# Hand-given SyncE order, a spectrum kept in SBUF, direct weight loads and deeper rings in a spectral-mixer and token-MLP kernel

## The chip, the core and the metric

The kernel runs on one core of a Trainium2 chip. The metric is the device time of one execution in microseconds, and a smaller number is better. The core's engines are TensorE (PE, the matrix unit), VectorE (DVE), ScalarE (ACT), GpSimd (POOL) and SyncE (SP). Here SyncE issues every data transfer. All transfers run on the core's 16 DMA engines.

## What is computed

The program computes a forward pass of two residual blocks and all its gradients except that of a constant input. The first block mixes with a two-dimensional real FFT of a normalised input of 2048 by 448, multiplied by a learned complex filter. The second is a token-mixing MLP across the 2048 rows.

```python
def _A_ref(x, w_r, w_i):
    X = jnp.fft.rfft2(x.astype(jnp.float32), axes=(-2, -1))
    X = X * (w_r + 1j * w_i)                    # w: 2048 x 225
    return jnp.fft.irfft2(X, s=(S, D), axes=(-2, -1)).astype(jnp.bfloat16)

def _B_ref(x, w1, b1, w2, b2):                  # w1: 2048 x 1792, w2: 1792 x 2048
    h = _layernorm(x, axis=-1)
    u = _gelu(jnp.einsum("bsd,sf->bdf", h, w1) + b1)
    y = jnp.einsum("bdf,fs->bds", u, w2) + b2
    return y.transpose(0, 2, 1)

h  = x + _A_ref(_layernorm(x), w_r, w_i)
h2 = h + _B_ref(_layernorm(h), w1, b1, w2, b2)
# outputs: h2 (out_0) and the gradients for x (out_1), w_r (out_2), w_i (out_3),
#          w1 (out_4), b1 (out_5), w2 (out_6), b2 (out_7), given grad_out
```

## The kernel before, in words

The transforms are matrix products with cosine and sine tables that the kernel makes at its start on VectorE, ScalarE and GpSimd (`Ut`, `Vt`, `UTt`, `VTt`, `csF`, `csI`, `Rm`, `RTm`). A length of 2048 is split into 16 times 128. The program runs through these stages:

1. **Forward row stage.** `prep_x` folds two of 16 row groups on VectorE, a DMA transpose makes `xT` (line 473), `d_stage` and `s1_stage` multiply it, and a DMA (line 495) writes the result across partitions into `D2`. Between these, `fill(n)` puts n products of `dg_gen` into TensorE's order: the gradient of the MLP's hidden layer, 14 groups of 16 products, each on a transposed block of w2 (line 188).
2. **Forward spectrum stage** (`s2_stage`). For each of eight pairs of groups, TensorE makes the spectrum X, `w_mult` multiplies by the filter on VectorE, and `s2_inv` transforms back. A DMA (line 542) writes the result into `D3`. X is also stored to DRAM (`xspec_d`, line 653), from a ring of two buffers.
3. **Inverse rows** (`inv_rows`) give h row by row, then its layer norm.
4. **u stage** (line 726): seven pairs of blocks of w1 (1 MB each, a ring of two), then the GELU and its derivative.
5. **y stage** (line 771): 16 rows against w2 in 0.9 MB pieces of two rows each (`load_w2c`, line 705, a ring of two).
6. **dh stage** (line 848): 16 rows against transposed blocks of w1 (line 828, a ring of three); the backward row stage runs among its rows (`d_pair`).
7. **Backward spectrum stage** with `bwd_mult`, which also forms the filter's gradient from the stored X and reads the filter from a packed DRAM copy (`w_d`, written at line 656, read at line 858).
8. **Inverse rows of the backward pass** (`gx_consumer`): each row ends in a store of a row group of out_1 (line 944).

From the end of stage 6 to the end, `fill` puts the 480 products of the two weight gradients (`gw2_gen` line 903, `gw1_gen` line 918) between the others. They read transposed slices (line 889, a ring of three, two loaded ahead).

TensorE's order is that of the program text. The order of all other engines, SyncE's included, is set by a scheduler at build time from its own model of time. An engine runs its instructions strictly in that order, so an issue on SyncE that waits holds all that stand behind it. `Ring.next()` gives buffers in turn. The small ring `r448` (8 buffers) holds the row temporaries of `ln_bwd`, so that a row's `tmp` takes the buffer from which the row before was stored.

## Time and profile before

| what | us |
|---|---|
| median of 3 runs | 479.72 (477.13 to 480.07) |
| the profiled execution, its own time | 482.09 |
| its span, first to last instruction | 479.7 |
| TensorE busy in the span (1920 products) | 376.4 |
| VectorE / ScalarE / GpSimd busy | 263.4 / 235.0 / 48.5 |
| moved by DMA | 89.73 MB, 187 GB/s on average |

Busy time is the time in which an engine had an instruction in work. An engine's idle time is put down to what ended it. The granted clock is the share of full speed at which TensorE was let run.

### The profile page before, as it was taken

The numbers are of one execution on the slowest core, as the hardware profiler recorded it, in microseconds if no ns is written. First come the engines' busy times: TensorE is split into PE (matmuls) and PEld (weight loads), VectorE is DVE, ScalarE is ACT, GpSimd is POOL, SyncE is SP. The second block draws the span as 40 slices with busy tenths as digits, with TensorE's granted clock in tenths as the row PEclk, the third lists the DMA queues.
The fourth block names the chain that finished last, engine by engine and source line by source line (L and its number), as shares of the span: only waits on it lengthen the run. The fifth ranks groups of instructions, "written<-read, shape, count | busy, mean of one in ns | idle before, by whom it ended". The sixth has DMA issues, their size and how long they took to land.

```text
span 479.7 us, 6024 instructions
## 1 busy us (share of the span) xinstructions
PE 376.4 (78%) x1920; PEld 190.3 (40%) x1920; DVE 263.4 (55%) x732; ACT 235.0 (49%) x478; POOL 48.5 (10%) x50
## 2 busy tenths in 40 slices
PE   1694577768698999918779899966999998589960
PEld 0252243324353545504335455532444454345530
DVE  9998572642287588821224877700167850235764
ACT  0674532454275545311222234553689885557771
POOL 6105997000000000000000000000000000000000
PEclk9998768979798999987999999997999998979995
DMA  8998969598794674287686999699757869967641
GB/s 230 252 193 175 180 138 265 145 222 209 195 238 183 169 202 139 53 195 194 190 226 113 202 194 195 139 193 287 206 183 209 232 177 223 137 197 168 211 166 57
DMA packets 173255, 89.73 MB, mean 187 GB/s; under 512 B 119081, under 2 KB 168233, under 8 KB 172841
## 3 DMA queue, kind: packets, MB, share of 16 engines
q1 hardware_dynamic: 173224, 89.36, 76.0%
q8 instruction: 15, 0.25, 0.2%
q14 instruction: 16, 0.12, 0.1%
HBM read 29.41 MB, written 25.74 MB: 115 GB/s over the span
## 4 chain that ended last, share of the span: by engine, by line
PE 38%; DMA 27%; DVE 18%; SPq 6%; ACT 4%; POOL 3%; issue 3%; DVEq 0%; ACTq 0%; POOLq 0%
DMA out_dram<-r_81 10%; PE ps_mm L903 8%; PE ps_mm L726 7%; PE ps_mm L848 6%; PE ps_mm L771 3%; PE ps_mm L918 3%; DMA xspec_d<-rS 3%; DVE stats L583 3%; PE ps_mm L603 3%; DMA r_73<-in_B_w_dram 2%; DMA out_dram<-rD 2%; POOL Ut L351 2%; DMA rst<-rE 2%; DVE r_81 L822 2%; SPq L857 2%
## 5 line engine op out<-in xcount | busy, mean ns | idle before, releaser
L603 PE MATMUL ps_mm<-rC,rE 128*128 128x448 bf16 x224 | 60.2, 403 | 14.2 <-DMA rE<-in_B_w_dram 8.0
L918 PE MATMUL ps_mm<-rC,rst 112*128 112x512 bf16 (+1 forms) x256 | 55.6, 367 | 6.3 <-DMA rst<-rB 6.3
L771 PE MATMUL ps_mm<-rE,rS 128*128 128x448 bf16 x224 | 45.2, 362 | 17.2 <-DMA rS<-in_B_w_dram 17.2
L903 PE MATMUL ps_mm<-rG,rst 112*128 112x512 bf16 x224 | 53.9, 390 | 4.2 <-DMA rst<-rE 4.2
L726 PE MATMUL ps_mm<-rB,r_72 128*128 128x448 bf16 x224 | 45.1, 362 | 2.5 <-DVE rB L685 1.7
L848 PE MATMUL ps_mm<-rD,r_73 128*128 128x448 bf16 x224 | 43.7, 352 | 1.1 <-DMA r_73<-in_B_w_dram 1.1
L603 PEld LDWEIGHTS <-rE 128*128 128x128 bf16 x224 | 24.1, 110 | 42.0 <-issue 20.9
L906 ACT CAST rO<-ps_mm 128x512 bf16<-128x512 f32 x56 | 32.0, 594 | 13.0 <-PE ps_mm L903 12.8
L771 PEld LDWEIGHTS <-rS 128*128 128x128 bf16 x224 | 22.0, 100 | 40.2 <-DMA rS<-in_B_w_dram 19.4
L918 PEld LDWEIGHTS <-rst 112*128 112x128 bf16 x256 | 25.1, 101 | 29.5 <-DMA rst<-rB 6.6
L921 ACT CAST rO<-ps_mm 128x512 bf16<-128x512 f32 (+1 forms) x60 | 30.0, 540 | 13.4 <-PE ps_mm L918 13.2
L903 PEld LDWEIGHTS <-rst 112*128 112x128 bf16 x224 | 22.3, 100 | 31.7 <-DMA rst<-rE 4.7
L783 ACT ACTIVATE r_81<-rC 128x448 bf16<-128x448 bf16 x16 | 9.2, 576 | 48.5 <-DVE r_81 L778 38.3
L726 PEld LDWEIGHTS <-r_72 128*128 128x128 bf16 x224 | 22.3, 100 | 25.1 <-issue 4.8
L778 DVE SCALAR_TENSOR_TENSOR r_81<-ps_mm,b2col,r_81 128x448 bf16<-128x448 f32 x16 | 10.8, 682 | 38.1 <-PE ps_mm L771 38.0
L564 PE MATMUL ps_ff<-csI,rAT 113*128 113x448 bf16 x128 | 31.3, 368 | 0.6 <-ACT rAT L553 0.5
L848 PEld LDWEIGHTS <-r_73 128*128 128x128 bf16 x224 | 21.7, 98 | 23.5 <-DMA r_73<-in_B_w_dram 2.2
L480 PE MATMUL ps_ff<-csF,rT 113*128 113x226 bf16 x64 | 13.0, 289 | 17.6 <-DMA rT<-rF 17.6
L553 ACT CAST rAT<-ps_ff 113x512 bf16<-113x512 f32 x32 | 18.4, 584 | 16.6 <-PE ps_ff L550 16.3
L486 ACT CAST r_78<-ps_ff 128x452 bf16<-128x452 f32 x32 | 17.1, 538 | 17.0 <-PE ps_ff L483 17.0
L816 ACT ACTIVATE r_81<-ps_mm 128x448 bf16<-128x448 f32 x16 | 8.7, 544 | 30.0 <-PE ps_mm L848 28.9
L513 ACT CAST rS<-ps_ff 128x452 bf16<-128x452 f32 x29 | 15.7, 540 | 15.1 <-DMA xspec_d<-rS 7.7
(198 smaller groups left out, 609.0 us busy)
## 6 DMA issues: line engine op xcount, KB each, us to landing
r_72<-in_B_w_dram SPq DMA_DIRECT2D x7, 1024.0 KB
rS<-in_B_w_dram SPq DMA_DIRECT2D x8, 896.0 KB
out_dram<-rO SPq DMA_DIRECT2D x14, 512.0 KB
out_dram<-rO SPq DMA_DIRECT2D x16, 448.0 KB
r_72<-r_78 SPq DMA_DIRECT2D x32, 113.0 KB
r_73<-r_78 SPq DMA_DIRECT2D x32, 113.0 KB
out_dram<-r_81 SPq DMA_DIRECT2D x32, 112.0 KB
w_d<-rG SPq DMA_DIRECT2D x1, 1808.0 KB
```

The costliest lines, as they stand in the source:

```text
L486: sc.copy(out=ab, in_=pv)
L513: evac(out=xc[:, i, :, :], in_=pv)
L553: sc.copy(out=aT[0:KC].rearrange("p a b -> p (a b)"), in_=pa[0:KC, :])
L564: nc.tensor.matmul(py[:, 0:D], lhsT=aT[0:KC, i, :], rhs=csI[0:KC, i // 2, i % 2, :], start=(i == 0), stop=(i == 3))
L603: nc.tensor.matmul(pg[:, 0:D], lhsT=wT[:, t, :], rhs=go_tp[:, t, :], start=(t == 0), stop=(t == NT - 1))
L726: nc.tensor.matmul(pu[:, 0:D], lhsT=w1c[:, t, jj * P:(jj + 1) * P], rhs=hln[:, t, :, :], start=(t == 0), stop=(t == NT - 1))
L771: nc.tensor.matmul(py[:, 0:D], lhsT=w2cs[t // 2][:, j, (t % 2) * P:(t % 2 + 1) * P], rhs=g_[:, j, :, :], start=(j == 0), stop=(j == NFB - 1))
L848: nc.tensor.matmul(pdh[:, 0:D], lhsT=wT[:, j, :], rhs=du[:, j, :, :], start=(j == 0), stop=(j == NFB - 1))
L903: nc.tensor.matmul(pw[:], lhsT=gt[0:DC, k, :], rhs=goT[0:DC, k, c * 512:(c + 1) * 512], start=(k == 0), stop=(k == 3))
L906: evac(out=o[:, c * 512:(c + 1) * 512], in_=pw[:])
L918: nc.tensor.matmul(pw[:, 0:n * P], lhsT=ht[0:DC, k, :], rhs=du_t[0:DC, 4 * c:4 * c + n, k, :], start=(k == 0), stop=(k == 3))
L921: evac(out=o[:, c * 512:c * 512 + n * P], in_=pw[:, 0:n * P])
```

## The change

The change takes SyncE out of the scheduler's hands: `manual_schedule` now names PE and SP, so transfers are issued in the order of the program text. To place them, `mm()` replaces every matmul call and adds up columns / 2400 us as a clock of TensorE's work. `defer(us, fn, *views)` puts a transfer into the text once that clock has moved on by `us`, or sooner, when one of its buffers is asked for again. A number of other edits go with it:

- `Xs` in a new region `rX` holds the spectrum from the forward to the backward pass; `xspec_d` and `w_d` are gone. The fold buffers share `rX` in the forward and `rS` in the backward pass, and `s2_stage` takes a lag `ml` (3 forward, 0 backward) between X and its product with the filter.
- The filter's 18 loads (16 partitions by 16 rows of 225 values each, most of them) move from the row stage to the start of the forward spectrum stage. In the backward pass the same 18 loads from `A_w_r` and `A_w_i` replace the one from `w_d`.
- Ring depths: w2's transposed blocks 5 instead of 3, w1's transposed blocks 4 instead of 3, weight-gradient slices 3 loaded ahead instead of 2.
- `grad_out` in its second layout, two w1 blocks and two row groups of h are loaded during the u stage (`after_u`), `goT` in the y stage's later rows, and `du_t` is transposed in four pieces. The filter gradient's 18 stores go out two per row of `gx_consumer`.

```diff
+    def defer(us, fn, *views):
+        ...
+        later.append((clock[0] + us, len(later), run))
+        ...
+        for v in views:
+            Ring.held.setdefault(id(v), []).append(run)
+    def mm(out, lhsT, rhs, start, stop):
+        nc.tensor.matmul(out, lhsT=lhsT, rhs=rhs, start=start, stop=stop)
+        clock[0] += int(np.prod(rhs.shape[1:])) / 2400.0
+        run_due()
-    ctx.enter_context(tc.manual_schedule(engines={mybir.EngineType.PE}))
+    ctx.enter_context(tc.manual_schedule(engines={mybir.EngineType.PE, mybir.EngineType.SP}))
-    w2T_ring = ring(rE, 0, 3, NT, P)
+    w2T_ring = Ring(ring(rE, 0, 3, NT, P).views + ring(rO, S, 2, NT, P).views)
 def dg_gen():
...
                 if t == NT - 1:
                     evac(out=dgu[:, j, :, :], in_=v4(pg[:, 0:D]))
+                    load_w2T()
 def s1_stage(s1, ab):
...
-        nc.sync.dma_start(out=D2[...], in_=cs)
+        defer(RESH_LAG, lambda: nc.sync.dma_start(out=D2[...], in_=cs), cs)
 def s2_stage(get_x, on_mult, ml, n_fill, gap):
+        flush()
...
-        lag = 2
+        lag = 2 + ml
...
-                ys.append(on_mult(c2, xc))
+            if ml <= c2 < nh + ml:
+                ys[c2 - ml] = on_mult(c2 - ml, xs[c2 - ml])
+    def fwd_x(c2):
+        for _ in range(6):
+            next(w_loads, None)
+        return Xs[:, 2 * c2:2 * c2 + 2, :, :]
     def fwd_mult(c2, xc):
-        nc.sync.dma_start(out=xspec_d[:, 2 * c2:2 * c2 + 2, :, :], in_=xc)
         return w_mult(c2, xc, W_view_F, False)
+    after_u = {0: [lambda: load_w2c(0)], 1: [lambda: load_w2c(1)], 2: [lambda: load_go_pt(0)],
+               3: [lambda: load_go_pt(1)], 4: [lambda: load_w1T(0)], 5: [lambda: load_w1T(1)],
+               6: [lambda: load_h(0), lambda: load_h(1)]}
 # y stage, after the products of row t
+        if t % 2 == 1 and t // 2 + 2 < NT // 2:
+            load_w2c(t // 2 + 2)
         y_tail(t, py)
         gb2_part(t)
+        if t in (2, 6):
+            load_w1T(2 + t // 4)
+        if t in (8, 10, 12, 14):
+            load_goT(t // 2 - 4)
-    nc.sync.dma_start_transpose(out=du_t.rearrange("p j b q -> p (j b) q"), in_=rD[:, 0:NFB * 4 * P])
-    nc.sync.dma_start(out=W_view_B, in_=w_d[:])
+    for q in range(4):
+        defer(4.0 * q, lambda q=q: nc.sync.dma_start_transpose(
+            out=du_t.rearrange("p j b q -> p (j b) q")[:, 14 * q:14 * q + 14, :], in_=rD[:, 14 * P * q:14 * P * (q + 1)]))
+    w_back = w_io(W_view_B, A_w_r, A_w_i, False, nc.sync)
+    def bwd_x(c2):
+        if c2 == 0:
+            gp_.memset(W_view_B[:, :, :, DF:KW], 0.0)
+        for _ in range(18):
+            next(w_back, None)
+        return X_ring.next()
     def bwd_mult(c2, xc):
-        xs = xs_ring.next()
-        nc.sync.dma_start(out=xs, in_=xspec_d[:, 2 * c2:2 * c2 + 2, :, :])
+        xs = Xs[:, 2 * c2:2 * c2 + 2, :, :]
 def gx_consumer(t, py):
-        xt = m448.next()
-        nc.sync.dma_start(out=xt, in_=x_pt[:, t, :])
+        for _ in range(2):
+            next(g_out, None)
+        xt = xts.pop(0)
+        if t + 1 < NT:
+            load_xt(t + 1)
...
-        nc.sync.dma_start(out=out_1[0].rearrange(...)[:, t, :], in_=gx)
+        defer(3.5, lambda: nc.sync.dma_start(out=out_1[0].rearrange(...)[:, t, :], in_=gx), gx)
```

**SyncE around the last `D2` stores of the forward row stage.** In the kernel before, `r_72<-r_78` (line 495) are these stores, `rG<-in_A_w` (line 433) the filter's loads, `rT<-rF` (line 473) the `xT` transposes, and `rE<-in_B_w` (line 188) the w2 blocks.

```order
L495 DMA r_72<-r_78 8x16x452
L433 DMA rG<-in_A_w_i_dram 16x16x225
L433 DMA rG<-in_A_w_i_dram 16x225
L495 DMA r_72<-r_78 8x16x452
L473 DMA_TRANSPOSE rT<-rF 128x8x128
L495 DMA r_72<-r_78 8x16x452 x2
L188 DMA_TRANSPOSE rE<-in_B_w_dram 128x16x128
L495 DMA r_72<-r_78 8x16x452 x4
L188 DMA_TRANSPOSE rE<-in_B_w_dram 128x16x128
L495 DMA r_72<-r_78 8x16x452
```

In the changed kernel the same place of SyncE's order reads as follows; line 553 is the `D2` store, line 489 the filter's loads and line 227 the w2 blocks.

```order
L553 DMA r_72<-r_77 8x16x452 x4
L227 DMA_TRANSPOSE rE<-in_B_w_dram 128x16x128
L553 DMA r_72<-r_77 8x16x452 x2
L227 DMA_TRANSPOSE rE<-in_B_w_dram 128x16x128
L489 DMA rG<-in_A_w_r_dram 16x16x225
L489 DMA rG<-in_A_w_r_dram 16x15x225
L489 DMA rG<-in_A_w_r_dram 16x16x225 x6
L489 DMA rG<-in_A_w_r_dram 16x225
L489 DMA rG<-in_A_w_i_dram 16x16x225
```

All 18 loads of the filter, of which the last nine begin here, now stand behind the last `D2` store and one w2 block, in one piece.

**VectorE at the first filter products.** In the kernel before, lines 526 to 530 are one pair's `w_mult`, line 513 is a copy of X out of PSUM, and lines 865 and 867 finish a row of scale factors, `srow`, after a GpSimd memset (line 863).

```order
L499 TENSOR_SCALAR r_72<-r_72 128x4x226 x4
L526 TENSOR_TENSOR rS<-rS,rG 128x904
L527 TENSOR_TENSOR rS<-rS,rG 128x904
L528 TENSOR_TENSOR rS<-rS 128x2x226
L530 TENSOR_TENSOR rS<-rS 128x2x226
L513 CAST rS<-ps_ff 128x452
```

In the changed kernel lines 586 to 590 are that `w_mult`, lines 948 and 950 finish `srow`, and line 962 is the scaling of X by `srow` for the backward pass.

```order
L558 TENSOR_SCALAR r_72<-r_72 128x4x226 x4
L948 TENSOR_TENSOR rO<-rO,srow 128x226
L950 TENSOR_TENSOR srow<-rO 128x226
L586 TENSOR_TENSOR rS<-rX,rG 128x904
L587 TENSOR_TENSOR rS<-rX,rG 128x904
L588 TENSOR_TENSOR rS<-rS 128x2x226
L962 TENSOR_TENSOR rX<-rX,srow 128x904
L590 TENSOR_TENSOR rS<-rS 128x2x226
```

The scaling by `srow` has moved from the backward to the forward spectrum stage, once per pair, and the two instructions that finish `srow` stand ahead of the first product.

**SyncE before the backward spectrum stage.** In the kernel before, `rC<-rD` (line 857) makes `du_t`, `rT<-rF` is the last `xT`, `rD<-w_d` the filter, `out_dram<-rO` (line 908) a store of out_6, and `rst<-rE` (line 889) a weight-gradient slice.

```order
L857 DMA_TRANSPOSE rC<-rD 128x56x128
L473 DMA_TRANSPOSE rT<-rF 128x8x128
L858 DMA rD<-w_d 128x7232
L908 DMA out_dram<-rO 128x2048
L495 DMA r_72<-r_78 8x16x452
L889 DMA_TRANSPOSE rst<-rE 128x4x128
```

In the changed kernel, at the point where the program text enters that stage, line 978 is the slice and line 997 the store of out_6.

```order
L978 DMA_TRANSPOSE rst<-rE 128x4x128
L997 DMA out_dram<-rO 128x2048
L489 DMA rD<-in_A_w_r_dram 16x16x225
L489 DMA rD<-in_A_w_r_dram 16x15x225
L489 DMA rD<-in_A_w_r_dram 16x16x225 x6
L489 DMA rD<-in_A_w_r_dram 16x225
L489 DMA rD<-in_A_w_i_dram 16x16x225
L489 DMA rD<-in_A_w_i_dram 16x15x225
L489 DMA rD<-in_A_w_i_dram 16x16x225 x6
L489 DMA rD<-in_A_w_i_dram 16x225
L978 DMA_TRANSPOSE rst<-rE 128x4x128
L997 DMA out_dram<-rO 128x2048
```

The filter's load has moved from ahead of the first stores of out_6 to behind the sixth, and one instruction has become 18.

## Rows read from the trace of the kernel before

**Rows 1.** Busy time by stage: from:to, length, each engine, PE clock, DMA share, GB/s.

```profile
151.30:195.30 44.00, 43.29 (x217) 21.53 (x217) 30.59 (x78) 23.14 (x31) 0.00 (x0) 0.96 0.57 171
195.30:257.60 62.30, 45.11 (x227) 22.04 (x225) 18.28 (x37) 11.90 (x31) 0.00 (x0) 0.92 0.69 178
257.60:310.20 52.60, 50.30 (x284) 27.33 (x282) 40.20 (x118) 21.21 (x58) 0.00 (x0) 1.00 0.91 176
310.20:347.00 36.80, 27.70 (x123) 12.66 (x122) 3.62 (x11) 19.49 (x37) 0.00 (x0) 0.91 0.90 222
347.00:402.20 55.20, 53.17 (x262) 25.23 (x260) 33.13 (x70) 44.83 (x90) 0.00 (x0) 1.00 0.71 203
402.20:463.40 61.20, 54.90 (x312) 29.64 (x312) 27.84 (x77) 41.08 (x93) 0.00 (x0) 0.92 0.80 179
```

**Rows 2.** Who waited for whom: total us, times, longest us.

```profile
PE ps_mm L771 <- DMA rS<-in_B_w_dram: 17.2, 5, 11.8
...
ACT rS L513 <- DMA xspec_d<-rS: 7.7, 4, 3.6
```

**Rows 3.** SyncE's timeline, forward part: start, us, instruction, how many.

```profile
58.47 1.37 SPq L433 DMA_DIRECT2D rG<-in_A_w_i_dram  x2
...
72.66 1.93 SPq L188 DMA_TRANSPOSE rE<-in_B_w_dram  x1
74.68 0.73 SPq L495 DMA_DIRECT2D r_72<-r_78  x1
```

**Rows 4.** Timelines of ScalarE, GpSimd and VectorE around the forward spectrum stage's start.

```profile
66.54 1.05 ACT L412 ACTIVATE r_73<-r_73 128x448 f32<-128x448 f32 x2 [4.36 <-DVE r_73 L227]
...
80.50 0.28 POOL L863 MEMSET rO<- 128x226 f32 x1
...
82.20 0.63 DVE L526 TENSOR_TENSOR rS<-rS,rG 128x904 bf16<-128x904 bf16 x1 [2.11 <-ACT rS L513]
...
84.02 0.62 DVE L513 CAST rS<-ps_ff 128x452 bf16<-128x452 f32 x1
```

**Rows 5.** The scaling by `srow`, line 873: shortest/median/longest ns, first and last start.

```profile
L873 DVE TENSOR_TENSOR rS<-rS,srow x8: 621/630/630, 255.6 to 384.8; 128x904 bf16<-128x904 bf16 x8
```

**Rows 6.** The chain that ended last, in order of time: start, us, what.

```profile
120.51 4.06 DMA r_73<-r_78
...
212.17 5.56 DMA rS<-in_B_w_dram
...
359.92 1.94 PE ps_mm L903 x9
...
408.14 6.96 DMA out_dram<-rD
```

**Rows 7.** TensorE's timeline around the backward spectrum stage's start: idle before and releaser in brackets.

```profile
324.16 0.56 PE L480 MATMUL ps_ff<-csF,rT 113*128 113x226 bf16 x2 [4.85 <-DMA rT<-rF]
...
334.08 13.05 PE L903 MATMUL ps_mm<-rG,rst 112*128 112x512 bf16 x52 [4.25 <-DMA rst<-rE]
346.97 0.36 PE L511 MATMUL ps_ff<-r_72,Ut 128*128 128x452 bf16 x1
...
356.67 0.35 PE L538 MATMUL ps_ff<-rS,UTt 128*128 128x452 bf16 x1
```

**Rows 8.** SyncE's timeline, backward part.

```profile
312.01 8.88 SPq L857 DMA_TRANSPOSE rC<-rD  x1
...
404.59 8.92 SPq L431 DMA_DIRECT2D out_dram<-rD  x12
```

**Rows 9.** VectorE's timeline: ends of rows 0, 3, 5 and 15 of out_1.

```profile
409.70 0.69 DVE L822 SCALAR_TENSOR_TENSOR r_81<-r_81,rstd_x,rA 128x448 bf16<-128x448 bf16 x1
...
433.16 0.69 DVE L822 SCALAR_TENSOR_TENSOR r_81<-r_81,rstd_x,rA 128x448 bf16<-128x448 bf16 x1
...
441.76 0.69 DVE L822 SCALAR_TENSOR_TENSOR r_81<-r_81,rstd_x,rA 128x448 bf16<-128x448 bf16 x1
...
476.52 0.69 DVE L822 SCALAR_TENSOR_TENSOR r_81<-r_81,rstd_x,rA 128x448 bf16<-128x448 bf16 x1
```

More of the change, by code (lines that the diff above doesn't have):

```diff
@@ L55, in next, with release @@
         self.i += 1
+        Ring.release(v)
         return v
+    @staticmethod
+    def release(v):
+        for run in Ring.held.pop(id(v), ()):
+            run()
 @with_exitstack
```

281 lines of the change are left out of this document (161 added, 120 removed).

## The prediction

> **What bounds the kernel now.** I cut the span into stages first. TensorE is busy 376.4 of 479.7 us, so it is the engine that everything else keeps waiting, and the question for each stage is which wait ends last there. From 257.6 to 310.2, and from 347.0 to 402.2, it is busy 50.3 of 52.6 and 53.2 of 55.2 us: there nothing is to be won. It is idle for 17 of 62.3 us in the y stage, and for 9 of 36.8 us ahead of the backward spectrum stage [rows 1]. The list of waits names transfers: the y stage waits 17.2 us, in five pieces, for blocks of w2, and ScalarE waits 7.7 us to write X because its ring still holds a store to DRAM [rows 2]. SyncE's timeline shows why: its issues stand in one line and take 0.6 to 2 us each [rows 3], and one du_t transpose occupies it for 8.88 us [rows 8] while TensorE waits 4.85 us for the `xT` behind it and 4.25 us for a slice [rows 7]. At the end, 12 small stores in one piece hold it for 8.92 us [rows 8], and the last row groups run out long after TensorE's last product at 463.4. So SyncE's order is a real cost, and the change goes at it. The sum is made against the profiled execution's span, 479.7, with 2.4 us around it in its own 482.09; the median of the runs, 479.72, is 2.4 below that execution, so span and median are one number here and I forecast the median.
>
> **A. To the first inverse row (124.6 now).** Now the last `D2` store is issued at 74.68 with the filter's loads ahead of it, at 0.69 us each [rows 3]. The order still puts ScalarE's last table (it ends at 67.6 [rows 4]) ahead of the last copies, so I place the last `D2` at 69.0. Behind it stand a w2 block, 1.93, and the 18 filter loads, 12.3 by 0.69: 83.2. The trace has no landing time of such a load; the nearest rows are 4.06 us for a `D3` store and 6.96 us for the filter-shaped stores [rows 6]. I take 4.06, as SyncE sends little beside them: the first product with the filter starts at 87.3. The lag of three pairs covers X, not this. `srow`'s two instructions now stand ahead of it and need GpSimd's memset, done at 80.8 [rows 4], so the loads are later and decide. One pair costs VectorE 1.82 us (82.20 to 84.02 [rows 4]), and now also the scaling by `srow`, 0.63 [rows 5]: 8 x 2.45 = 19.6, to 106.9. Then 1.5 for the last pair's products and copies (an estimate from 0.36 and 0.62 per instruction [rows 4, 7]), 0.7 and 4.06 for the `D3` store: 113.2. The ring wait on `xspec_d`, 7.7 us, is inside this. Gain **11.4**. Bounds: 5.6, if both landings take 6.96; 17.9, if the filter has landed by 80.8. The 18 products that move from the inverse rows into this stage cost nothing: TensorE waits for VectorE there anyway, and VectorE paces the inverse rows, so that stretch keeps its length.
>
> **B. The u stage.** TensorE needs 43.3/7 = 6.2 us per pair of blocks [rows 1]. For four of them SyncE now sends a w1 block and another 0.9 MB: 1.97 MB. The stages' GB/s over their DMA shares, 171/0.57 and 178/0.69, give 300 and 258 GB/s at full share [rows 1], so 6.6 to 7.6 us. With a ring of two the overshoot, 0.4 to 1.4 each, comes out at TensorE. I take **-2**; bounds 0 (the first pair's slack absorbs it) and -5.6.
>
> **C. The y stage.** A w2 piece takes 5.56 us from issue to landing [rows 6]; TensorE works 45.1/8 = 5.64 us on a pair of rows [rows 1]. In the new order the issue stands right behind the products that free its buffer. The third piece still comes late: after row 1 there are only 16 of a pair's 28 products left, 3.2 us, so 2.4 are waited. The other five miss by 5.56 + 0.4 of issue - 5.64 = 0.3 each, 1.6. The `goT` transposes, now beside the last two pieces, I put at 2. That leaves 6 of 17.2: gain **11**. Bounds: 3 (each load at 6.96), 15 (only the third late).
>
> The Trainium skill (DMA: Bandwidth & Descriptors, section Anatomy of one DMA) fits a transfer, issued from GpSimd there, as 2.0 us plus bytes at 436 GB/s; for 0.92 MB that is 4.1 us, an estimate, where the row shows 5.56. By the rule the y stage would wait 2.9 and the sum below would be 447.
>
> **D. From 310.2 to the backward spectrum stage.** What TensorE must do there is 100 weight-gradient products at 1.94/9 [rows 6] = 21.6 us and four groups of the row stage, 2.3. The first slices were loaded during the u stage; now their issue follows the last `xT` but one, so I count 2.4 us for a landing. `du_t` in four pieces of 2.2 no longer stands ahead of the last `xT`. 26.3 instead of 36.8 [rows 1]: gain **10.5**. Bounds: 5.6 (the 4.85 of `xT` remains), 12.9 (slices in time).
>
> **E. The backward filter loads: a new wait.** Now the filter arrives long before its use. In the new order its 18 loads stand behind the sixth store of out_6, which needs the 96th of those 100 products: they can't begin before the spectrum stage does. TensorE reaches the first inverse product 9.7 us after the stage's start (346.97 to 356.67 [rows 7]). The loads need 12.3 + 4.06, then 1.82 on VectorE and 0.6 on ScalarE: 18.8. A stall of **-9**. Behind the 18 on SyncE stand the next slices, but three lie ready (10 us of products). Bounds: -8; and -13, if the loads behave as the 12 stores of that shape (0.74 each, 6.96).
>
> The Trainium skill (same page, section Specifications) asks for at least 512 bytes per piece for line rate, and a row of 225 bf16 values is 450. That speaks for the -13 end, with which the sum would be 454.
>
> **F. The backward inverse rows.** Now 77.5 us from 402.2. Row 0 ends 8.2 in, but row 3 only at 433.85, behind the 12 stores; from row 5 to row 15 a row takes 3.48 (442.45 to 477.21), 2.5 follow the last [rows 9]. That pace is not TensorE's, it is a ring: a row's `tmp` waits for the store of the row before. The change doesn't lengthen that ring, and spreads 18 stores over 9 rows. For those rows I take 4.3, the pace of rows 3 to 5, when SyncE and the queues were loaded [rows 9]: 8.2 + 8 x 4.3 + 7 x 3.48 + 2.5 = 69.5. Gain **8**. Bounds: 2 (5 us a row), 14.6 (3.48 throughout).
>
> **Sum.** 11.4 - 2 + 11 + 10.5 - 9 + 8 = 30, so 479.7 - 30 = **450**. The dh stage is left as it is: the deeper w1 ring has 1 us of waits to remove.
>
> **Rivals.**
> *The DMA engines bind* (0.22). Their share is already 0.69 to 0.91 in most stages [rows 1], and deeper prefetch moves bytes closer together. If each landing is 1.5 us longer: 3 in A, 9 over the six pieces of C, 1.5 in E, 4 in F: 467.
> *The transfers are hidden* (0.22). 5.4 of 89.7 MB vanish (`w_d` and `xspec_d` at 1.8 each written, `xspec_d` read; the 18 loads replace `w_d`'s read). If landings become 1.5 us shorter: 3 in A, 3 in C, 1.5 in E, 3 in F (rows at 3.9): 439. The skill's fit named in C points this way; no row has yet shown it.
> *The last rows become SyncE's* (0.06), the slower side. Each of nine rows adds two stores, 1.4 us, to about 2.5 us of other issues, all in one line with the store that the next row's `tmp` waits for. For it: while SyncE was held, rows 0 to 3 took 7.8 each [rows 9]. Against: 3.9 us fit nearly into a row, and VectorE's own wait covers them. It decides at (69.5 + 34.7 - 10.7)/15 = 6.2 us a row on average; from there the kernel is at 484.5 or more.
>
> **How the numbers follow.** The forecast holds 0.5 and the three rivals 0.22, 0.22 and 0.06. A change of 1% is about what a measurement of this kernel can tell from none, 475 to 484.5. Slower is the last rival, 0.06; the same is the far end of the first, 0.04 (all its terms at their bounds); faster 0.90. The range 436 to 467 takes in the two larger rivals and leaves out the far ends and the slower one, 2 in 10 together.
>
> **What would show it.** Right: `D3`'s last landing near 113 and the u stage's start near 140; the y stage's waits for w2 near 6; the backward filter loads issued as the spectrum stage starts, with TensorE waiting about 9 us for ScalarE's negated Y; a row of out_1 every 4.3, then 3.5 us. Wrong: a first forward filter product much later than 87, w2 pieces that land in over 7 us, or out_1 rows over 6 us apart.

## The result, and the profile after

The changed kernel takes 464.46 us in the median of its runs (462.36 to 469.85), the kernel before 478.43 beside it (476.25 to 480.07): a ratio of 0.970, 95% interval 0.963 to 0.976. The forecast was 450, with a range of 436 to 467. The 469.85, and a 469.13 in one experiment below, are single slow runs that the ratios leave out. So the direction came as forecast and the time lies in the range, but only about half of the gain came: some 14 us of the 30 that were summed up did not. The profiled execution has a span of 463.0 us (own time 464.73), against 479.7 before.

The page of the changed kernel, first the busy times, then the total traffic. TensorE has its 1920 products as before; 370.3 us of work are now 80% of a shorter span.

```profile
PE 370.3 (80%) x1920; PEld 187.3 (40%) x1920; DVE 261.9 (57%) x725; ACT 239.7 (52%) x485; POOL 51.8 (11%) x54
...
DMA packets 175144, 84.18 MB, mean 182 GB/s; under 512 B 123272, under 2 KB 170376, under 8 KB 174984
```

The same cut by stages as in [rows 1] (from:to, length, busy time of PE, PEld, DVE, ACT and POOL with counts, PE clock, DMA share, GB/s): inverse rows with the start of the u stage, u, y, dh, the stretch ahead of the backward spectrum stage, that stage, and the backward inverse rows up to TensorE's last product.

```profile
114.39:137.90 23.51, 18.93 (x137) 11.23 (x138) 20.85 (x63) 14.55 (x28) 0.00 (x0) 1.00 0.36 118
137.90:181.40 43.50, 42.83 (x216) 21.53 (x216) 29.85 (x74) 23.69 (x33) 0.00 (x0) 0.96 0.85 256
181.40:234.60 53.20, 43.22 (x226) 21.51 (x224) 18.40 (x37) 11.82 (x31) 2.73 (x3) 1.00 0.90 218
234.60:286.00 51.40, 50.19 (x285) 27.64 (x283) 39.12 (x116) 19.34 (x54) 0.00 (x0) 1.00 0.88 175
286.00:318.56 32.56, 26.52 (x122) 12.04 (x120) 3.51 (x10) 18.62 (x36) 0.25 (x1) 0.90 0.88 195
318.56:386.19 67.63, 56.41 (x262) 26.12 (x261) 30.72 (x64) 45.75 (x89) 0.00 (x0) 0.92 0.56 169
386.19:449.80 63.61, 55.28 (x313) 29.22 (x311) 28.05 (x80) 46.31 (x104) 0.00 (x0) 0.92 0.64 177
```

Read against [rows 1], length by length, this gives the account of the change. Every boundary is the same event in both kernels.

| stretch | before | after | gain | forecast |
|---|---|---|---|---|
| start to the first inverse row (A) | 124.6 | 114.4 | +10.2 | +11.4 |
| inverse rows, start of u | 26.7 | 23.5 | +3.2 | 0 |
| u stage (B) | 44.0 | 43.5 | +0.5 | -2 |
| y stage (C) | 62.3 | 53.2 | +9.1 | +11 |
| dh stage | 52.6 | 51.4 | +1.2 | 0 |
| to the backward spectrum stage (D) | 36.8 | 32.6 | +4.2 | +10.5 |
| that stage (E) | 55.2 | 67.6 | -12.4 | -9 |
| backward inverse rows to the end (F) | 77.5 | 76.8 | +0.7 | +8 |
| sum | 479.7 | 463.0 | +16.7 | +30 |

So A, B and C together with the two stretches beside them gave 24.2, where 20.4 was forecast; what is missing lies behind 286 us, in D, E and F, which gave -7.5 instead of +9.5. The experiments go there first, then at SyncE's order as a whole.

### The profile page after: what moved, and what is told of

Its sections match the earlier page's. It is cut to its first block, busy times and chain, and to the rows that moved or that the text cites. A ratio compares the mean times of both kernels' runs of the same rounds, so it can differ in the third digit from the quotient of the medians.

```text
span 463.0 us, 6021 instructions
## 1 busy us (share of the span) xinstructions
PE 370.3 (80%) x1920; PEld 187.3 (40%) x1920; DVE 261.9 (57%) x725; ACT 239.7 (52%) x485; POOL 51.8 (11%) x54
## 4 chain that ended last, share of the span: by engine, by line
PE 44%; DVE 18%; DMA 18%; SPq 8%; ACT 6%; POOL 3%; issue 2%; DVEq 0%; ACTq 0%; POOLq 0%
PE ps_mm L151 36%; PE ps_ff L151 8%; SPq L489 5%; DMA out_dram<-r_80 5%; DMA r_80<-h_d 4%; DVE stats L644 3%; POOL Ut L403 2%; DVE r_80 L911 2%; DMA r_80<-in_A_x_dram 2%; DMA r_72<-in_B_w_dram 1%; DMA rst<-rE 1%; DMA rS<-in_B_w_dram 1%; DVE r_73 L298 1%; DMA rst<-rB 1%; DVE rB L682 1%
## 5 line engine op out<-in xcount | busy, mean ns | idle before, releaser
L151 PEld LDWEIGHTS <-rst 112*128 112x128 bf16 x480 | 47.4, 101 | 68.7 <-issue 11.4
L151 PE MATMUL ps_mm<-rC,rst 112*128 112x512 bf16 (+1 forms) x256 | 56.3, 367 | 10.9 <-DMA rst<-rB 8.7
L151 PE MATMUL ps_mm<-rE,rS 128*128 128x448 bf16 x224 | 43.4, 353 | 10.0 <-DMA rS<-in_B_w_dram 10.0
L151 PE MATMUL ps_mm<-rC,rE 128*128 128x448 bf16 x144 | 37.7, 399 | 9.8 <-DMA rC<-in_grad_out_dram 8.9
L151 PEld LDWEIGHTS <-r_73 128*128 128x128 bf16 (+1 forms) x352 | 33.9, 111 | 27.6 <-issue 3.5
L151 PEld LDWEIGHTS <-rS 128*128 128x128 bf16 (+1 forms) x288 | 27.7, 98 | 35.3 <-DMA rS<-in_B_w_dram 12.2
L151 PEld LDWEIGHTS <-r_72 128*128 128x128 bf16 x224 | 22.3, 100 | 26.3 <-issue 6.5
L151 PEld LDWEIGHTS <-rE 128*128 128x128 bf16 x144 | 15.4, 107 | 29.6 <-issue 12.2
L151 PE MATMUL ps_ff<-rS,UTt 128*128 128x452 bf16 x32 | 12.1, 379 | 15.1 <-ACT rS L592 15.1
L613 ACT CAST rAT<-ps_ff 113x512 bf16<-113x512 f32 x32 | 18.5, 590 | 8.4 <-PE ps_ff L151 8.4
L906 DVE CUSTOM_DVE_ANT_0 r_80<-r_80 128x448 bf16<-128x448 bf16 x16 | 10.0, 624 | 22.6 <-ACT r_80 L905 15.4
L151 PE MATMUL ps_mm<-rC,rO 128*128 128x448 bf16 x80 | 20.5, 380 | 1.1 <-DMA rO<-in_B_w_dram 1.1
L586 DVE TENSOR_TENSOR rS<-rS,rD 128x904 bf16<-128x904 bf16 x8 | 5.0, 630 | 28.1 <-DMA rD<-in_A_w_i_dram 16.9
```

The costliest lines, as they stand in the source:

```text
L151: nc.tensor.matmul(out, lhsT=lhsT, rhs=rhs, start=start, stop=stop)
L613: sc.copy(out=aT[0:KC].rearrange("p a b -> p (a b)"), in_=pa[0:KC, :])
L906: ve.tensor_tensor_reduce(out=w(junk), in0=w(pb), in1=nrm, scale=m2scale, scalar=0.0, op0=ALU.mult, op1=ALU.add, accum_out=m2)
```

## The experiments

Each experiment starts from the changed kernel. "After" below is its 464.46 us, its ratio 0.970. The kernel before ran at 478.43 beside the changed kernel, but at 480.88 beside e1 to e4 and at 482.06 beside e5 to e8 (the numbers stand in the labels of the expectations). So differences of medians make these gains 2 to 4 us too small if that drift is real, and ratios to the kernel before, a hundredth of which is 4.8 us, are the firmer comparison.

### The ring of the last rows: gx in buffers of its own

In the backward inverse rows each row takes five slots of the eight-slot ring r448, in the order xt, gx, pb, junk, tmp. Counted through, `tmp` of a row lands on the slot of the `gx` of the row before, and so waits for that row's store to out_1. The list of VectorE's waits in the changed kernel's last stage (waited for, total us, times, longest):

```profile
DVE r_80 L909 <- DMA out_dram<-r_80: 20.8, 14, 3.6
```

```
+    gx_ring = ring(rX, 0, 4, D)
 ...
-        gx = m448.next()
+        gx = gx_ring.next()
```

> The gradient rows gx of the last stage get four buffers of their own in rX (free once the backward products are done) instead of slots of the eight-slot ring r448. Theory 'store in the loop': with five slots taken per row out of eight, the product tmp of row t lands in the slot that gx of row t-1 left, so each row waits for the store of the row before (DVE L909 waited 20.8 us for out_dram<-r_80 in 14 rows), and the 4.4 us per row fall to the 3.5 to 3.7 us that TensorE's share of a row takes: 16 rows by 0.7 to 0.9 is 11 to 14 us less, end 451 to 455. Rival 'SyncE's line': the rows are late because xt loads, slices and filter-gradient stores stand in one order on SyncE; then L909's wait goes but the xt loads (ACT L1041 waited 11.6 us) take its place and the time stays at 462 to 466. Rival 'transfers': stores and slices share the DMA engines, 458 to 462.

Measured: 457.19 us (455.92 to 459.06), ratio 0.949 [0.942, 0.955]: 7 us less. The wait is gone, and what VectorE waits for instead stands one step further up: ScalarE's normalised row of x.

```profile
DVE r L906 <- ACT r L1042: 19.3, 11, 3.4
```

The first row of out_1 to the last, which took 393.6 to 459.4 in the changed kernel, takes 396.3 to 452.3 here: 56.0 instead of 65.8 us. The first copy of the backward inverse rows, which lies ahead of the edit, starts 2.7 us later here (389.6 for 386.9), so the rows themselves won 9.8 us; the shift also shows how far one trace can differ from another. The store in the loop is shown as a cause. It isn't the whole: 3.73 us a row is still not what the rows reach without x in the way, as the next run shows, and the end is 457, not 451 to 455.

### The same, with x loaded three rows ahead

```
+    gx_ring = ring(rX, 0, 4, D)
+    xt_ring = ring(rX, 4 * D, 4, D)
 ...
-    load_xt(0)
+    load_xt(0)
+    load_xt(1)
+    load_xt(2)
 ...
-        if t + 1 < NT:
-            load_xt(t + 1)
+        if t + 3 < NT:
+            load_xt(t + 3)
```

> As e1_gx_ring, and the rows of x come into four more buffers of rX, loaded three rows ahead instead of one. With the store out of the loop, ACT still waited 12.7 us in 12 rows for x rows whose issue stands on SyncE behind the store of the row before. Theory 'x rows late': these waits go and the rows run at TensorE's pace of 3.5 us, 3 to 6 us less than e1_gx_ring (457.2): 451 to 454. Rival: the rows are held by TensorE and the evictions on ACT by now, 456 to 458.

Measured: 453.61 us (453.07 to 453.74), ratio 0.941 [0.935, 0.946]: 10.9 less than after by the medians, 14 by the ratios. The rows go from 395.8 to 448.5, 3.51 us each, the pace that was forecast for TensorE. VectorE no longer waits for a normalised x at all, though ScalarE still has some waits for x rows in the list (11.8 us in 10). Rows 0, 8 and 15 of out_1 in VectorE's timeline, first of the changed kernel (start, us, instruction):

```profile
393.61 0.69 DVE L911 SCALAR_TENSOR_TENSOR r_80<-r_80,rstd_x,rA 128x448 bf16<-128x448 bf16 x1
...
434.09 0.69 DVE L911 SCALAR_TENSOR_TENSOR r_80<-r_80,rstd_x,rA 128x448 bf16<-128x448 bf16 x1
...
459.44 0.69 DVE L911 SCALAR_TENSOR_TENSOR r_80<-r_80,rstd_x,rA 128x448 bf16<-128x448 bf16 x1
```

and of the kernel with both rings:

```profile
395.83 0.69 DVE L911 SCALAR_TENSOR_TENSOR rX<-r,rstd_x,rA 128x448 bf16<-128x448 bf16 x1
...
424.92 0.68 DVE L911 SCALAR_TENSOR_TENSOR rX<-r,rstd_x,rA 128x448 bf16<-128x448 bf16 x1
...
448.48 0.69 DVE L911 SCALAR_TENSOR_TENSOR rX<-r,rstd_x,rA 128x448 bf16<-128x448 bf16 x1
```

The first eight rows, the ones that also send the 18 filter-gradient stores, go from 5.06 us each to 3.64, though those stores and their bytes are all still there in the same places. So what the stores move does not hold these rows; they were held by having to wait for a store and an x row, and in the changed kernel these stood behind other issues on SyncE.

### The backward filters issued earlier

The changed kernel loads the filter into rD inside the backward spectrum stage. In this experiment it goes into r3, free since the last dh row (the inverse rows' `D3` goes to rD), and SyncE issues a piece behind every four products from `d_pair(6)` on.

```
-    W_view_B = cut(rD, 0, NG, 2, KW)
+    W_view_B = cut(r3, 0, NG, 2, KW)
 ...
-    fill(N_FILL_B[1])
+    for _ in range(4):
+        fill(4)
+        next(w_back, None)
     d_pair(7)
     s1_stage(*abq.pop(0))
-    fill(N_FILL_B[2])
+    for _ in range(15):
+        fill(4)
+        next(w_back, None)
```

> The backward filters go to r3 (free since the last dh row) and the backward inverse rows' D3 to rD, so the 18 filter loads needn't wait for the du transposes; SyncE issues them one behind every four products in the stretch ahead of the backward spectrum stage. Theory 'place': the loads are late only because they are issued inside the stage; DVE's first product no longer waits (16.9 and 5.2 us now), TensorE's 8.6 us wait for the negated Y and the slow clock behind it go, and the end comes 7 to 10 us earlier, 454 to 457. Rival 'SyncE is full': the 18 issues cost 12.6 us of SyncE whose line ahead of the stage is already 30 of 32.5 us long, so slices and D2 pieces slip by as much as the stage gains: 462 to 467.

Measured: 461.39 us (459.25 to 469.13), ratio 0.956 [0.949, 0.963]. TensorE's waits from 285 to 400 us, in the changed kernel:

```profile
PE ps_ff L151 <- ACT rS L592: 8.6, 1, 8.6
PE ps_mm L151 <- DMA rst<-rE: 5.2, 1, 5.2
PE ps_mm L151 <- DMA rst<-rB: 2.6, 1, 2.6
```

and in this kernel:

```profile
PE ps_mm L151 <- DMA rst<-rE: 9.7, 3, 7.8
```

Both theories are half right. The 8.6 us behind ScalarE's negated Y are gone, so an earlier place is enough to remove them; 4.5 of them came back as a longer wait for slices of g, since the loads stand ahead of those slices on SyncE. ScalarE's first copy of the backward inverse rows starts 5.5 us earlier (381.4 for 386.9), but the last row of out_1 only 4.7.

### The filters as one packed piece

The packed copy of the kernel before is brought back: stored to DRAM behind the first two w1 loads, and read in one piece at the place where the 18 are issued.

```
+    nc.sync.dma_start(out=w_d[:], in_=W_view_F)
 ...
-        for _ in range(18):
-            next(w_back, None)
+            nc.sync.dma_start(out=W_view_B, in_=w_d[:])
```

> The packed copy of the filters is brought back: one store of rG to DRAM behind the first two w1 loads in the forward half, one load at the place where the 18 pieces are issued now. Theory 'place': the load still waits for its place at the stage's start; a transfer of 1.85 MB in one piece took the kernel before about as long as there, so TensorE's wait shrinks only by the difference between 12.6 us of issues and one transfer of some 9 us (issue 0.6 us): 3 to 5 us less, and the store costs 0 to 3 in the forward half; 460 to 464. Rival 'pieces': the 450-byte rows are the cost, the wait disappears almost whole, 454 to 458.

Measured: 463.03 us (462.48 to 463.46), ratio 0.961 [0.956, 0.966]: 1.4 less by the medians, and the intervals of the two ratios overlap. In the trace TensorE's wait for the negated Y shrinks from 8.6 to 3.8 us. On SyncE's and VectorE's timelines the load is issued in 1.33 us and landed when the first product starts, some 8 us after that; in the changed kernel the 18 issues take 12.6, and the first pair's second product, which needs the last of them, starts at 334.84.

```profile
319.50 1.33 SPq L955 DMA_DIRECT2D rD<-w_d  x1
...
329.16 0.63 DVE L587 TENSOR_TENSOR rS<-rS,rD 128x904 bf16<-128x904 bf16 x1 [17.20 <-DMA rD<-w_d]
```

So packing takes about 5 us off that wait, and the place leaves the other 4. The time is inside the 460 to 464 of 'place'. In the traces the first copy of the backward inverse rows starts 4.0 us earlier (383.0) and the last row of out_1 2.6 (456.8); the last experiment looks for where such a gain goes.

### The first slices of g, earlier

```
+        if t in (12, 13, 14):
+            first3.append(load_slice(rE, t - 12))
 ...
-        ahead = [load(0), load(1), load(2)]
+        ahead = first3 if reg is rE else [load(0), load(1), load(2)]
```

> The first three slices of g for the w2 gradient are loaded in dh rows 12 to 14 instead of behind the last dh row. Theory 'the line of SyncE bounds the stretch': SyncE's line from 282.9 to 313 is filled by three slices (3.9 us), the du transposes (9.7 us), D2 pieces and stores, and TensorE's 5.2 us wait for a slice at 312.2 is the end of that line; 3.9 us less of it give 3 to 4.5 us, 460 to 461.5. Rival 'the ring of three': the slices' own round trip through three buffers sets the pace and the wait stays: 463.5 to 465.5.

Measured: 463.53 us (463.12 to 465.12), ratio 0.962 [0.957, 0.968]: about 1 us less by the medians, 3.5 by the ratios, and the two intervals overlap, so the times don't decide. TensorE's wait for a slice ahead of the backward spectrum stage falls from 5.2 to 1.8 us, as the theory of the full line has it, and ScalarE's first copy of the backward inverse rows starts at 382.5 instead of 386.9. The last row of out_1 starts at 457.8 instead of 459.4: of 4.4 us, 1.6 are left. SyncE's line in the changed kernel; by the chain of work that ended last, the slice that was waited for is the one issued at 308.57, landed 3.58 us later:

```profile
282.86 3.90 SPq L978 DMA_TRANSPOSE rst<-rE  x3
286.80 2.93 SPq L939 DMA_TRANSPOSE rC<-rD  x1
...
304.53 3.23 SPq L939 DMA_TRANSPOSE rC<-rD  x1
...
308.57 1.19 SPq L978 DMA_TRANSPOSE rst<-rE  x1
```

### A third buffer for the w2 pieces

```
-    w2c_ring = ring(rS, 0, 2, NFB, 256)
+    w2c_ring = Ring(ring(rS, 0, 2, NFB, 256).views + ring(rO, 0, 1, NFB, 256).views)
 ...
-               6: [lambda: load_h(0), lambda: load_h(1)]}
+               6: [lambda: load_h(0), lambda: load_h(1), lambda: load_w2c(2)]}
 ...
-        if t % 2 == 1 and t // 2 + 2 < NT // 2:
-            load_w2c(t // 2 + 2)
+        if t % 2 == 1 and t // 2 + 3 < NT // 2:
+            load_w2c(t // 2 + 3)
```

> The ring of w2 pieces in the y stage gets a third buffer in rO, which nothing else uses in that stage, and each piece is loaded one pair of rows earlier. Theory 'late issue': TensorE's 10.0 us of waits on w2 pieces (five, 1.35 to 2.97 us) are pieces issued a pair of rows too late behind the goT transposes; with one more pair of lead they go, 6 to 10 us less, 455 to 459. Rival 'bandwidth': the y stage is limited by what its transfers move, so the waits shrink to a third less at most, 461 to 465.

Measured: 460.03 us (459.33 to 462.75), ratio 0.955 [0.950, 0.961]. TensorE's waits in the y stage, in the changed kernel and then here:

```profile
PE ps_mm L151 <- DMA rS<-in_B_w_dram: 10.0, 5, 3.0
```

```profile
PE ps_mm L151 <- DMA rS<-in_B_w_dram: 3.0, 2, 1.6
```

7.0 of 10.0 us are gone, so these pieces came late because they were issued late, not because the DMA engines could not bring them. The end gains 4.4 us by the medians, 7 by the ratios.

### SyncE's order given back to the scheduler

```
-    ctx.enter_context(tc.manual_schedule(engines={mybir.EngineType.PE, mybir.EngineType.SP}))
+    ctx.enter_context(tc.manual_schedule(engines={mybir.EngineType.PE}))
```

> Only the hand-given order of SyncE is taken back: the scheduler orders SyncE again, everything else (X kept in SBUF, filters loaded from DRAM, the longer rings) stays. Theory 'order': the gain of 16 us lies in the order, so the time goes back to 474 to 484 or beyond, with the first inverse row, the y stage or the stretch ahead of the backward spectrum stage later than now. Rival 'rings and dropped copies': these carry the gain, 462 to 468.

Measured: 458.39 us (455.52 to 460.92), ratio 0.951 [0.945, 0.957]. The interval does not touch that of the changed kernel (0.963 to 0.976): the hand-given order as it stands makes the kernel some 6 us slower than the scheduler's order would, 9 by the ratios. My theory fell; even the rival put it too high. So the change's gain comes from the edits beside the order (the spectrum kept in SBUF, the deeper rings and the others). No run takes these apart, but for the direct backward loads, without which the kernel was no slower (e4); nor was the hand order run without them. By the traces the two orders trade stages:

| | hand order | scheduler's |
|---|---|---|
| first copy of the inverse rows | 114.8 | 121.0 |
| first row of y | 188.7 | 196.5 |
| first copy of the backward inverse rows | 386.9 | 386.7 |
| last row of out_1 | 459.4 | 452.3 |

Up to the first inverse row the hand order is 6.2 us ahead. The copies of `D3` begin at the same time in both (91.50 and 91.19), but in the changed kernel's timeline of SyncE all 16 stand in one piece, and in the scheduler's, shown second, other loads go out among them: a block of w1 behind the first two, two pieces of w2 among the last three, and grad_out right behind.

```profile
91.50 19.98 SPq L602 DMA_DIRECT2D r_73<-r_77  x16
```

```profile
94.44 0.62 SPq L735 DMA_DIRECT2D r<-in_B_w_dram  x1
95.71 11.29 SPq L602 DMA_DIRECT2D r<-r  x11
107.11 0.42 SPq L769 DMA_DIRECT2D rS<-in_B_w_dram  x1
107.63 1.96 SPq L602 DMA_DIRECT2D r<-r  x2
109.69 0.44 SPq L769 DMA_DIRECT2D rS<-in_B_w_dram  x1
110.23 3.91 SPq L602 DMA_DIRECT2D r<-r  x1
114.23 1.59 SPq L778 DMA_DIRECT2D rC<-in_grad_out_dram  x2
```

The time is lost at the last copy. TensorE's products ahead of the inverse rows end 0.9 us earlier under the scheduler (112.9 for 113.9), but the last copy is held until 114.1, where the hand order has issued it by 111.5, and TensorE goes on only at 120.33. (The profile puts this wait down to the load of grad_out, but the products read `D3`.) From 107 us on the DMA engines' share is 0.95, then 1.05 there; in the hand order it is 0.34 until the last copy is issued. Whether the late issue or the other bytes weigh more was not tried.

Between y and the backward inverse rows the scheduler wins 8.1 back, and in the rows 6.9: it loads the first slices of g at 156 to 165 us, long before the stretch that waits for them, and 13 of the 18 filter-gradient stores have gone by 400 us, where the hand order sends two with each row until 429. That these two are the cause is read from the traces; the early slices were tried apart (e3), the stores were not. One more thing is in the scheduler's trace: TensorE's waits for w2 in the y stage, 10.0 us in the hand order, are shorter with the scheduler's.

```profile
PE ps_mm L151 <- DMA rS<-in_B_w_dram: 8.2, 4, 4.0
```

### All of it together

Both rings of the last rows, three w2 buffers, the early slices, the filter early into r3 but issued by ScalarE, and the du transposes 7 us apart instead of 4.

```
-    w_back = w_io(W_view_B, A_w_r, A_w_i, False, nc.sync)
+    w_back = w_io(W_view_B, A_w_r, A_w_i, False, nc.scalar)
 ...
-        defer(4.0 * q, lambda q=q: nc.sync.dma_start_transpose(
+        defer(2.0 + 7.0 * q, lambda q=q: nc.sync.dma_start_transpose(
```

> Together: gx and x rings (e7), three w2 buffers (e6), first slices in the dh rows (e3), backward filters early into r3 (e2) but issued by ACT, so that SyncE's line is not lengthened, and the du transposes 7 us apart instead of 4. If the causes are separate stretches their gains add: e1 -7.3, e2's stage part -5.5, e3 -1 to -4, e6 0 to -8, e7 0 to -5 against 464.5 give 436 to 450. If what is left is TensorE's own work (370 us busy of 463) and the transfers, each gain is partly given back later: 450 to 455. If ACT's 18 issues hold up its evictions, over 455.

Measured: 435.31 us (435.05 to 437.78), ratio 0.904 [0.899, 0.909], 29 us under the changed kernel. It is just below the 436 to 450 in which the gains of the single edits add up. By the medians the four edits alone had come to 10.9 + 4.4 + 0.9 + 3.1 = 19.3 (e7, e6, e3, e2), 10 less than together; by the ratios to the kernel before, they come to 0.029 + 0.015 + 0.008 + 0.014 = 0.066, and together to 0.970 - 0.904 = 0.066. So that they give more together than apart is not shown; the firmer comparison has them add up, with the later du transposes and ScalarE's issues among what was changed. In the traces the first copy of the backward inverse rows starts 17.2 us earlier (369.7) than in the changed kernel, and the time from there to the last row of out_1 is 12.2 less, so nothing of the first is given back in the second. Of TensorE's waits in the last stage one kind is left:

```profile
PE ps_mm L151 <- ACT rO L1015: 4.9, 8, 1.1
```

### Three turns of the best version

The same kernel with SyncE's order given to the scheduler:

> All edits of e8_all_act, and SyncE's order given back to the scheduler. With the rings as the change left them the scheduler's order was faster than the hand order (e5 458.4 against 464.5): 6 us lost up to the first inverse row, 8 won up to the first backward inverse row, 7 won in the last rows. Theory 'the hand order lost only where its loads came late': e8 has mended those places, so the scheduler now only loses the 6 us of the forward half: 439 to 443. Rival 'the scheduler orders better everywhere but there': 428 to 434. Rival 'the scheduler sees none of the new slack': over 445.

Measured: 435.38 us (433.10 to 438.28), ratio 0.909 [0.902, 0.915]: no difference from e8 that can be told, and between the ranges of the theory (439 to 443) and of its first rival (428 to 434). The first copy of the inverse rows is again late, 120.8 for 113.6, and 371.3 for 369.7 in the backward half; the end is the same. With the buffers and issues in place it no longer matters to the end who orders SyncE.

With SyncE issuing the 18 backward loads:

> All edits of e8_all_act, but SyncE issues the 18 backward filter loads (one behind every four products) as in e2. Theory 'SyncE's line ahead of the backward spectrum stage is full': its 12 us of issues come back as waits on slices or D2 pieces, 4 to 9 us more than e8's 435.3: 439 to 444. Rival: with the slices loaded early and the du transposes spread there is room, 434 to 437.

Measured: 435.00 us (433.26 to 438.48), ratio 0.908 [0.902, 0.914]. The rival is right: once the slices are early and the du transposes spread, SyncE has the room, and the queue that issues the filters is no part of the gain.

With the forward filters issued by ScalarE, meant to be early:

> All edits of e8_all_act, and the 18 forward filter loads are issued by ACT, two behind each of the rows 7 to 15 of the forward spectrum, in place of SyncE in the first pairs of the spectrum stage. In e8 DVE's first product waited 12.9 us for the last of them and TensorE 5.1 us for the negated Y behind it. Theory 'the same lateness as in the backward half': the wait of TensorE goes, 4 to 5 us less: 430 to 432. Rival 'the stretch up to there is bound by the w2 transposes' transfers' (DMA share 0.73): the loads push those, 434 to 438.

Measured: 440.42 us (439.37 to 444.10), ratio 0.920 [0.914, 0.925]: 5 slower than e8, and slower than theory (430 to 432) and rival (434 to 438) had it. TensorE's wait for the negated Y is gone as meant, but ScalarE's order is the scheduler's, and it moved the loads to the very start, where they stand beside the first pieces of x, grad_out and w2:

```profile
4.68 5.22 ACTq L489 DMA_DIRECT2D rG<-in_A_w_r_dram  x4
```

TensorE's waits for grad_out and w2 (in `rE`) up to 115 us, 8.9 and 2.1 in e8, became 12.6 and 7.2. That the early loads cause this is read from the trace, not tried.

```profile
PE ps_mm L151 <- DMA rC<-in_grad_out_dram: 12.6, 3, 9.4
PE ps_mm L151 <- DMA rE<-in_B_w_dram: 7.2, 2, 3.7
```

### Where the gain of the early slices went

> The edits of e3_slices_early and of e7_gx_xt_rings in one kernel. Alone, e3 brought the first backward inverse row 4.4 us earlier (386.9 to 382.5) and the end only about 1 us; e7 left that row where it was and brought the end 11 us earlier. Theory 'the rows' own loop gave the gain back': with the rows no longer bound by their stores and x rows, the 4.4 us reach the end: about 449. Rival 'the work ahead of the end is fixed': the gain of e3 is lost in any case, 452 to 454.

(Its edits are those of e3 and e7.) Measured: 447.50 us (445.01 to 451.24), 6.1 less than e7 by the medians; but the kernel before also ran 3.6 lower beside it (478.45 for 482.06), and the two ratios are both 0.941 (here [0.934, 0.947]). The times alone don't settle it. The traces lean to the first theory: the first copy of the backward inverse rows starts 4.6 us ahead of e7's (382.7 for 387.2) and the last row of out_1 6.1 ahead (442.4 for 448.5), whereas in e3 only 1.6 of 4.4 were left at that row. It is one trace each, and in e1 the first copy moved by 2.7 us with no edit ahead of it, so this too is not settled.

## Why the prediction was right, and where it was off

**The premise, not borne out.** The prediction begins with SyncE's order as the cost that the change goes at. With that order alone handed back the kernel is not slower than the changed one but 6 us faster, so with those edits in place the hand order takes away from the gain. By stage the order gives 6.2 of the 10.5 us by which the first copy of the inverse rows moved (125.3 before, 121.0 with the scheduler's order, 114.8 with the hand order). In the y stage, where the place of the issue was the reason given, it gave no less waiting: the waits for w2 are 8.2 us with the scheduler's order and 10.0 with the hand order. Which of the edits beside the order carries that stage stays open. That the time lies in the range is luck in part: D, E and F together came out 17 us short, and 3.8 us of it was made up ahead of them by gains that were not forecast; without these the time would have been about 468, outside the range.

**A, right.** The first product with the filter was forecast for 87.3 and started at 86.79; a pair was to take 2.45 on VectorE, `srow`'s scaling among it, and the first four start 2.5 to 2.6 apart. TensorE's last wait for `D3` is 0.53 us, so the landing was at about 114 where 113.2 was forecast. Two misses cancel in this: the 18 loads were issued by 84.3 instead of 83.2, and the last landed 2.5 us behind instead of 4.06. VectorE's timeline:

```profile
86.79 0.63 DVE L586 TENSOR_TENSOR rS<-rX,rG 128x904 bf16<-128x904 bf16 x1 [8.72 <-DMA rG<-in_A_w_i_dram]
...
89.34 0.63 DVE L586 TENSOR_TENSOR rS<-rX,rG 128x904 bf16<-128x904 bf16 x1
```

The 3.2 us more in the rows behind it were not forecast: I had them keep their length, because VectorE paces them. In the kernel before, TensorE's 5.4 us wait for the last copy of `D3` ends at the first of these rows, and behind it the granted clock is 0.50, the lower of its two levels, so VectorE gets its first row 3.4 us behind that product; in the changed kernel the clock is 1.00 from the start and it gets it 2.1 us behind. How the other 1.8 us come about, the 18 products fewer among them, is not shown. The kernel before:

```profile
124.60:128.00 3.40, 3.39 (x17) 2.08 (x18) 0.00 (x1) 1.60 (x3) 0.00 (x0) 0.50 1.14 300
```

**B**, forecast -2, came out at +0.5, just past its bound of 0: TensorE's only wait for w1 there is a single 0.52 us, so the loads kept up with the products.

**C, near in size, not in its reason.** The waits for w2 fell from 17.2 [rows 2] to 10.0, not to 6, and not because of the order, as the waits are no longer with the scheduler's order. That the stage still lost only 1.9 of the 11 is luck: its products took 43.2 us at a clock of 1.00, where they had taken 45.1 at 0.92 [rows 1], which was not in the sum. There are five of 1.4 to 3.0 us. I had the third piece as the only one with a large wait and gave the others 0.3 each; the third buffer shows that lead was what they lacked (3.0 left). A piece itself took 5.36 us to land, about the 5.56 of [rows 6].

**D, the step that failed most in the mechanism.** I counted `du_t` out, since it no longer stands ahead of the last `xT`, and gave 2.4 us for the first slices' landing. The forecast was 26.3 us, 23.9 of them work at full clock and 2.4 of waiting; it took 32.6, 26.5 busy and 6.0 idle. The four `du_t` pieces stayed on the same line, among copies of `D2`, slices and stores, and it is a *later* slice that waits for them, 5.24 us at 312.2. Behind that wait 20 products take 6.52 us, where 20 of 1.94/9 each are 4.3, at a granted clock of 0.67 up to the stage's start; that is most of the extra work.

```profile
312.20 6.52 PE L151 MATMUL ps_mm<-rG,rst 112*128 112x512 bf16 x20 [5.24 <-DMA rst<-rE]
```

The lower bound, 5.6, was for `xT` staying late and still too high: 4.2. The early slices and the trade of e2 show that SyncE's line bounds this stretch.

**E, right in mechanism and place, 3.4 too small.** From the stage's start to the first inverse product I forecast 18.8 us, and it took 18.5 (318.56 to 337.07). The last nine loads are issued by 332.44, and the first pair's second product on VectorE starts 2.4 us later:

```profile
326.63 5.81 SPq L489 DMA_DIRECT2D rD<-in_A_w_i_dram  x9
...
334.84 0.63 DVE L587 TENSOR_TENSOR rS<-rS,rD 128x904 bf16<-128x904 bf16 x1 [5.19 <-DMA rst<-rE]
```

The profile puts that product's wait down to a slice, but its operand is `rD`, the filter. TensorE's stall is 8.64:

```profile
337.07 0.53 PE L151 MATMUL ps_ff<-rS,UTt 128*128 128x452 bf16 x1 [8.64 <-ACT rS L592]
...
337.77 3.33 PE L151 MATMUL ps_mm<-rG,rst 112*128 112x512 bf16 x9
341.71 2.10 PE L151 MATMUL ps_mm<-rG,rst 112*128 112x512 bf16 x9
...
367.64 1.03 PE L151 MATMUL ps_mm<-rC,rst 112*128 112x512 bf16 x2 [2.57 <-DMA rst<-rB]
```

What was not in the sum: 2.57 us later in the stage for the first slices of hln, which the hand order loads only when the second weight gradient begins; and 3.2 us more of work, 56.4 for 53.2, at a clock of 0.92 for 1.00 [rows 1]. The group of nine products behind the stall alone runs 1.2 us longer, at a granted clock of 0.61, and from 367.6 to 372.0 the clock is 0.62. Against this stand 2.0 us of idle time that the kernel before had in the stage: 8.64 + 2.57 + 3.24 - 2.03 = 12.4. I had looked at the slices for g that lie ready, not at the change from one gradient to the next, and at no price of a stall beyond its length. The packed load says how the stall is divided: some 5 go with packing, 4 stay with the place.

**F, the term that was mis-sized.** I had the ring right (`tmp` waits for the store of the row before) and put eight rows at 4.3 and seven at 3.48. They took 5.06 and 3.62, which is 0.76 x 8 + 0.14 x 7 = 7.1 of the 7.3 that are missing. Not evenly: two of the eight took 8.5 and 8.1 us, the other six 4.0 on average. I thought the two stores a row would fit beside the ring; they stand in the ring, because the store that `tmp` waits for and the next x row stand behind them, and behind slices that wait for a free buffer, on one engine. SyncE's line at the first long row: row 2 is done at 402.4, and its store goes out at 405.73, behind a slice, two filter stores and an x row, among others.

```profile
403.72 1.25 SPq L487 DMA_DIRECT2D out_dram<-rD  x2
405.02 0.61 SPq L1030 DMA_DIRECT2D r_80<-in_A_x_dram  x1
405.73 0.40 SPq L1044 DMA_DIRECT2D out_dram<-r_80  x1
```

My bound of 5 us a row was the right value. The row I took 4.3 from, 3 to 5 of [rows 9], was the best stretch among the loaded ones: the first eight rows of the kernel before had taken 5.3 each. And 3.48 is not the ring's pace, as I read it, but about what the rows take without that ring: 3.51 with gx and x in buffers of their own.

**The rivals.** "The DMA engines bind" gives nearly the measured time (467) for the wrong reason: it lengthened every landing, but where a row can be compared they didn't get longer. In the chain that ended last, a `D3` copy takes 3.06 us for the 4.06 before and a w2 piece 5.36 for 5.56 [rows 6].

```profile
110.86 3.06 DMA r_73<-r_77
...
223.76 5.36 DMA rS<-in_B_w_dram
```

The filter's pieces had landed 2.4 us after the last issue, where I took 4.06, and w2's waits went with a third buffer. "The transfers are hidden" has the `D3` copy and the filter's landing on its side, but wanted the same in C and F, and there it did not come: a w2 piece landed 0.2 us sooner, and the loaded rows of out_1 took 5.06, not 3.9. "The last rows become SyncE's" named the right place and engine for what F lost, at 5.06 us a row in the loaded part, below the 6.2 from which it decides.

**The fit of a transfer and the short rows.** The Trainium skill's fit (DMA: Bandwidth & Descriptors, section Anatomy of one DMA) gave 4.1 us for a w2 piece, an estimate, and with it 2.9 us of waits in the y stage; the trace has 5.36 and 10.0, so for this stage the fit was the worse guide of the two. What the Trainium skill asks for at least, 512 bytes per piece (same page, section Specifications), spoke for the -13 end of E. E came out at -12.4, but not by the terms of that end: the pieces landed 2.4 us behind the last issue, not 6.96, and the stall was 8.64; the rest is the second wait and the clock. About 5 us of TensorE's wait went when 18 pieces became one, and the runs don't separate the length of their rows from their number.

## What to carry to other kernels

When an order is written by hand, a resource that loops through it (here the ring slot of gx, then the x row behind its store) sets the pace of the whole loop; give such a loop its own buffers before giving it an order. A gain ahead of a loop that is bound by itself can be lost in it: in single traces 8.2, 5.5, 4.4 and 4.0 us at the first backward inverse row (e6, e2, e3, e4) were 5.8, 4.7, 1.6 and 2.6 at the last row of out_1, though the times don't settle it, and by the ratios the edits add up. Compare such edits by their ratio to a kernel that ran beside them: by medians of different occasions the same edits gave 19 us apart and 29 together. And compare a hand order with the scheduler's own before crediting it: here the hand order was worth 6 us in one stage and cost 15 in others, the gain came from what was changed beside it, and with enough lead in the buffers neither order was better.
